# Scores of the first four head pairs as float32 products on TensorE, with the ranks of the plan set anew

## The chip, the cores and the metric

One Trainium2 chip, one NeuronCore. The time is the device time of one execution in microseconds (us); the kernel before is given as the median of three runs. Engines: PE (TensorE) does matrix products and PEld its weight loads, DVE (VectorE) and ACT (ScalarE) work element by element, POOL (GpSimd) helps, SP issues DMAs. PE writes only to PSUM; DVE and ACT read it from there.

## The reference

q, k and v are float32 of shape (4, 8, 1152, 64): 4 batches, 8 heads, 1152 positions, 64 numbers each. The weights come as float64, 512 x 2048 and 2048 x 512.

```python
q_pool = q.reshape(B, H, S // 2, 2, D).mean(axis=3)            # 576 queries
scores = 1 / np.sqrt(D) * np.matmul(q_pool, k.transpose(0, 1, 3, 2))
scores = scores - np.max(scores, axis=-1, keepdims=True)
attn = np.exp(scores)
attn = attn / (np.sum(attn, axis=-1, keepdims=True) + 1e-09)
attn_out = np.matmul(attn, v)                                  # (4, 8, 576, 64)
x = attn_out.transpose(0, 2, 1, 3).reshape(B * S, H * D)       # 2304 x 512
h = x @ w_in                                                   # 2304 x 2048
g = h * (1.0 / (1.0 + np.exp(-1.702 * h)))
out = g @ w_out                                                # 2304 x 512
```

## The kernel before

Two heads make a pair P, so there are 16 pairs, 4 to a batch. A pair has 9 score tiles n of 128 queries by 1152 keys: 4 of head A, 4 of head B, and one (L) with 64 queries of each. Each tile goes through S (scores on PE, L580), M (row maximum and copy out of PSUM on DVE, L589) and E (exp with row sum on ACT, L596). One PSUM area `s` of three banks holds the scores, so S of the next tile waits for M of this one.

Precision comes from splitting. For every pair the largest |q| and |k| are found (`q_max` L406, `k_max` L412), brought to all rows by a transpose on PE, a maximum, and a product (`rows_max` L421, `spread` L425 and L426, `to_all` L429), and turned into scales that are powers of two (`qk_scale`, L250 to L256 and L437). q and k times their scale are cut into two float16 parts (`q_hi`, `k_hi` on ACT by L240; `q_lo` L448, `k_lo` L462 on DVE), and both are transposed by a DMA each (`q_tr` L473, `k_tr` L469). A score tile is then six float16 products of 384 columns.

After E there are two ways. Seven pairs (WHOLE: 0, 1, 2, 3, 6, 10, 14) stay in float32: nine transposes of 128x128 on PE through the banks `o0` and `o1` (X, `w_tr` L655), three evictions of 384 columns (Y, `w_ev`, L240), float32 products with v (`w_pv` L678), and a product that spreads the reciprocal sums along rows (`w_rows` L693, evicted by `w_spread`). The other nine cut the probabilities into two float16 parts (H on ACT, L on DVE at L616), transpose them by DMA (T, `p_tr` L630) and multiply in float16 (`pv` L643). Row sums get 1e-9 added (D, `denom` L601) and are inverted (R, `recip` L608), tile by tile.

Beside this the float64 weights are decoded in 32 pieces (`w_load`, `w_exp`, `w_low` L275, `w_bits` L279, `w_sign` L285, `w_mul` L289 on POOL, `w_sum` L294 on PE) through four `raw` buffers, and cut into float16 parts (`w_hi`, `w_lo` L312). The MLP runs over nine blocks of 256 rows with eight steps each: 24 products of 256 columns (h, L840), tanh, gate and split on ACT and DVE, 12 products of 512 columns (o, L876). A block needs the x of all four pairs of its batch; the tanh of the first block waits for all 32 weight pieces.

The order on all engines is worked out before the launch by a list planner (class Plan): each task has an engine, a cost in us, the tasks and buffers that it waits for, and a rank; among tasks that could start within `wait` us of the earliest one on an engine, the lowest rank goes first. `rank` holds the numbers that the ranks are made of, `movable` names kinds of tasks that may go to a second engine. The plan only fixes the order of instructions per engine; on the chip they wait for semaphores.

Of the kernel before, what the change touches and what calls it, by code (L numbers as in the profile page):

```python
# [21 lines left out]
class Plan:  # L22
# [15 lines left out]
    def add(self, name, eng, cost, rank, fn, after=(), take=(), use=(), dma=0.0, or_on=None, two=False):  # L38
        t = dict(name=name, rank=rank, fn=fn, take=list(take), dma=dma, two=two)
# [19 lines left out]
    def order(self):  # L59
# [12 lines left out]
        dma_free, lock, out = 0.0, 0.0, []  # L72
# [17 lines left out]
        while len(out) < len(self.tasks):  # L90
# [13 lines left out]
            cost = t["on"][eng]  # L104
            end = free[eng] = self.run_pe(s, cost) if eng == "PE" else s + cost
# [12 lines left out]
            for h in heirs.get(t["name"], ()):  # L118
                for e in h["on"]:
                    at = free[e] if e == eng == "PE" and not t["dma"] else seen  # L120
# [10 lines left out]
def kernel(  # L131
# [38 lines left out]
    WHOLE = (0, 1, 2, 3, 6, 10, 14)  # L170


    rank = dict(
        w1=65.6152, w1_rate=1.375516, w2=121.4095, w2_rate=0.041077, w1_cut=225.7614,
        w1_cut_rate=0.0234, w2_cut=136.659, w2_cut_rate=1.877582, v_max=117.7693, load=-0.0554,
        prep=1.4415, max=-3.6165, exp=-72.3267, p_hi=0.5721, p_lo=1.4833, pv=17.7389, x=63.2346,
        recip=-10.7343, w_tr=2.6166, w_ev=-51.7958, g=-131.2414, pv_b=-6.1948, max_b=8.382,
        p_lo_b=-88.3476, prep_b=-1.6277, v=7.8426,
    )
    movable = dict(DVE=("x", "w_exp", "w_sign", "w_hi"), POOL=("denom",))  # L180
    wait = dict(PE=0.051, ACT=0.076, DVE=0.083, POOL=3838.461)
# [29 lines left out]
    w_r = const.tile([128, NJ * len(WHOLE), 2], F32, name="w_r")  # L211
# [111 lines left out]
    for i in range(32):  # L323
# [5 lines left out]
        plan.add(("w_load", i), "SP", 0.6, r - 2, lambda i=i: w_load(i), take=[("raw", raw)], dma=1.8)  # L329
        plan.add(  # L330
            ("w_exp", i), "ACT", act(512), r, lambda e, i=i: w_exp(e, i), [("w_load", i)], use=[raw], two=True,
# [20 lines left out]
    for c in range(8):  # L352
        for h in range(2):
# [9 lines left out]
            plan.add(("w_lo", c, h), "DVE", dve(1024), r, lambda c=c, h=h: w_lo(c, h), [("w_hi", c, h)], two=True)  # L363
# [9 lines left out]
    ORDER = [("A", 0), ("A", 1), ("B", 0), ("B", 1), ("A", 2), ("A", 3), ("B", 2), ("B", 3), ("L", 0)]  # L373
# [26 lines left out]
    def q_add(g, eng):  # L400
        raw, s = T["qraw", g.P], new("qs", ("qs", g.P), [128, NJ, D], F32)
        eng.tensor_tensor(out=s, in0=raw[:, :, 0, :], in1=raw[:, :, 1, :], op=ALU.add)
# [14 lines left out]
    def rows_max(m, key):  # L417
# [3 lines left out]
        nc.tensor.transpose(ps[0:n, 0:128], m, idf)  # L421

    def spread(key, n):
        r, d = new("cm", ("cm",) + key, [2, 1], F32), new("cd", ("cd",) + key, [2, 2], F32)
        nc.vector.tensor_reduce(out=r[0:n], in_=T[key][0:n, 0:128], axis=AX.X, op=ALU.max)  # L425
        nc.vector.tensor_scalar(out=d[0:n, 0:n], in0=idf[0:n, 0:n], scalar1=r[0:n], scalar2=None, op0=ALU.mult)  # L426

    def to_all(key, n):
        nc.tensor.matmul(  # L429
            out=T[key][:, 128:128 + n], lhsT=ones_f[0:n], rhs=T[("cd",) + key][0:n, 0:n], start=True, stop=True  # L430
        )

# [41 lines left out]

    def vm_load(b, i):
# [12 lines left out]
    def vm_scale(b):  # L488
        pow2(T["vma", b][:, 128:129], 2.0 ** -40, 14, s_v[:, b:b + 1], i_v[:, b:b + 1])
# [21 lines left out]
    for b in range(B):  # L511
        first = min(g.n0 for g in pairs if g.b == b)
        for i in range(H):
            r = first - 16 + 1.5 * i if b else -2 + i * 0.25
            plan.add(("vm_load", b, i), "SP", 0.6, r - 2, lambda b=b, i=i: vm_load(b, i),
# [9 lines left out]
        plan.add(("rows_max",) + va, "PE", 0.1, r - 20, lambda b=b, va=va: rows_max(T["vm", b], va), [("vm_row", b)],  # L525
                 take=[("tr", va)])
        plan.add(("spread",) + va, "DVE", 0.35, r - 20, lambda va=va: spread(va, 1), [("rows_max",) + va], use=[va])
        plan.add(("to_all",) + va, "PE", 0.15, r - 20, lambda va=va: to_all(va, 1), [("spread",) + va], use=[va])
        plan.add(("vm_scale", b), "DVE", 0.8, r, lambda b=b: vm_scale(b), [("to_all",) + va], use=[va])

    for g in pairs:
# [7 lines left out]
        plan.add(("q_load", G), "SP", 2.4, n0 + rank["load"], lambda g=g: q_load(g), gate, take=[("qraw", qr)], dma=1.4)  # L539
        plan.add(("k_load", G), "SP", 1.2, n0 + rank["load"] + 0.1, lambda g=g: k_load(g), gate, take=[("kraw", kr)], dma=2.2)  # L540
        plan.add(("q_add", G), pe[0], dve(576) if now else gps(576), r, lambda g=g, e=pe[1]: q_add(g, e),
                 [("q_load", G)], take=[("qs", qs)], use=[qr], two=True)
        plan.add(("q_max", G), "DVE", dve(576), r, lambda g=g: q_max(g), [("q_add", G)], use=[qs])
        plan.add(("k_max", G), "DVE", dve(1152), r, lambda g=g: k_max(g), [("k_load", G), ("q_max", G)], use=[kr])
        qa = ("qka", G)
        plan.add(("rows_max",) + qa, "PE", 0.1, r - 20, lambda g=g, qa=qa: rows_max(T["qk", g.P], qa),
                 [("q_max", G), ("k_max", G)], take=[("tr", qa)])
        plan.add(("spread",) + qa, "DVE", 0.35, r - 20, lambda qa=qa: spread(qa, 2), [("rows_max",) + qa], use=[qa])
        plan.add(("to_all",) + qa, "PE", 0.15, r - 20, lambda qa=qa: to_all(qa, 2), [("spread",) + qa], use=[qa])
        plan.add(("qk_scale", G), "DVE", 0.8, r, lambda g=g: qk_scale(g), [("to_all",) + qa], use=[qa])  # L550
        plan.add(("q_hi", G), "ACT", act(1152, ptr=1), r, lambda e, g=g: q_hi(e, g), [("qk_scale", G)],
                 take=[("qn", qk)], use=[qs], two=True, or_on=on("q_hi", DVE=dve(1152, fast=True)))
        plan.add(("q_lo", G), "DVE", dve(576), r, lambda g=g: q_lo(g), [("q_hi", G)], use=[qs, qk], two=True)
        plan.add(("k_hi", G), "ACT", act(1152, ptr=1), r, lambda e, g=g: k_hi(e, g), [("qk_scale", G)],
                 take=[("kn", kn)], use=[kr], two=True, or_on=on("k_hi", DVE=dve(1152, fast=True)))
        plan.add(("k_lo", G), "DVE", dve(1152), r, lambda g=g: k_lo(g), [("k_hi", G)], use=[kr, kn], two=True)
        plan.add(("q_tr", G), "SP", 3.0, r, lambda g=g: q_tr(g), [("q_lo", G)], take=[("qT", qt)], use=[qk], dma=2.7)
        plan.add(("k_tr", G), "SP", 3.0, r, lambda g=g: k_tr(g), [("k_lo", G)], take=[("kT", kt)], use=[kn], dma=2.7)
# [7 lines left out]
        plan.add(("v_lo", G), "DVE", dve(1152), r, lambda g=g: v_lo(g), [("v_hi", G)],  # L566
                 use=[("vraw", G), ("vhl", G)], two=True)


    def scores(n):  # L570
        g, kind, t = tile_of[n]
        ps = new("s", ("s", n), [128, 3, 512], F32, psum)
# [24 lines left out]

    def denom(e, n):
        whole = tile_of[n][0].whole
        r = T["rc", n] = w_r[:, WHOLE.index(n // NJ) * NJ + n % NJ, :] if whole else new("rc", ("rc", n), [128, 2], F32)  # L600
        (nc.vector if e == "DVE" else nc.gpsimd).tensor_scalar(  # L601
            out=r[:, 0:1], in0=T["sum", n], scalar1=1e-9, scalar2=1.0 if whole else 2.0 ** -15,
            op0=ALU.add, op1=ALU.mult,
# [30 lines left out]
    def pv(g, u, part):  # L634
# [5 lines left out]
        for c in range(KR):  # L640
            for a in range(2):
                pt, o = (T["pt", g.P, "AB"[a], u], 0) if u < 2 else (T["pt", g.P, "L", 0], 64 * a)
                nc.tensor.matmul(  # L643
                    out=ps[64 * a:64 * (a + 1), 0:w], lhsT=T["vhl", g.P][:, a, c, m],
# [374 lines left out]
```

## Time and profile before

| what | value |
|---|---|
| median of three runs | 840.02 us (838.73 to 841.5) |
| span of the profiled execution, first to last instruction | 841.4 us |
| PE busy | 779.7 us (93%) |
| PEld busy | 516.3 us (61%) |
| DVE busy | 628.5 us (75%) |
| ACT busy | 574.6 us (68%) |
| POOL busy | 99.7 us (12%) |

The profile is of one execution, whose time is not given apart from its span; the span lies 1.4 us above the median of the runs. Busy times are records of instructions. The matrix products overlap in their pipeline, so PE counts as busy from the start of a product until its end is out, and a PE that is shown busy is not always at its full rate: how far apart two products start says more.

### The profile page before, as it was taken

The numbers are of one execution on the slowest core, as the hardware profiler recorded it, in microseconds if no ns is written. First come the engines' busy times: TensorE is split into PE (matmuls) and PEld (weight loads), VectorE is DVE, ScalarE is ACT, GpSimd is POOL, SyncE is SP. The second block draws the span as 40 slices with busy tenths as digits, with TensorE's granted clock in tenths as the row PEclk, the third lists the DMA queues.
The fourth block names the chain that finished last, engine by engine and source line by source line (L and its number), as shares of the span: only waits on it lengthen the run. The fifth ranks groups of instructions, "written<-read, shape, count | busy, mean of one in ns | idle before, by whom it ended". The sixth has DMA issues, their size and how long they took to land.

```text
span 841.4 us, 16413 instructions
## 1 busy us (share of the span) xinstructions
PE 779.7 (93%) x6565; PEld 516.3 (61%) x6565; DVE 628.5 (75%) x1160; ACT 574.6 (68%) x892; POOL 99.7 (12%) x141
## 2 busy tenths in 40 slices
PE   1689999998979999999998999999989999999997
PEld 0356555556656765666665766666667657666664
DVE  5788998999999769798998589988975683222221
ACT  3588989998867778677766787786868774232322
POOL 1233232230001100010100010101110000000000
PEclk9999999999999999999999999999999999999999
DMA  8876965819999918999999559999893383000001
GB/s 284 247 187 209 250 151 166 210 61 205 216 172 210 215 49 168 181 185 209 215 212 212 111 109 198 174 202 199 158 216 67 43 174 80 14 13 13 17 10 25
DMA packets 296364, 126.96 MB, mean 151 GB/s; under 512 B 267360, under 2 KB 277600, under 8 KB 296288
## 3 DMA queue, kind: packets, MB, share of 16 engines
q1 hardware_dynamic: 296288, 125.92, 69.3%
q8 instruction: 51, 0.84, 0.4%
q14 instruction: 25, 0.20, 0.1%
HBM read 54.53 MB, written 4.72 MB: 70 GB/s over the span
## 4 chain that ended last, share of the span: by engine, by line
PE 64%; DVE 16%; DMA 9%; ACT 6%; issue 4%; SPq 1%; POOL 0%; ACTq 0%; DVEq 0%; POOLq 0%
PE h L840 17%; PE o L876 16%; PE s L580 11%; PE pv L678 6%; PE o L655 6%; PE pv L643 5%; DVE p L589 4%; DMA pt<-hl 4%; DVE hl L616 3%; DMA vst<-in_v_dram 2%; ACT p L596 2%; DMA ptl<-hl 2%; ACT pt L240 1%; DVE gf L854 1%; DVE raw L279 1%
## 5 line engine op out<-in xcount | busy, mean ns | idle before, releaser
L596 ACT ACTIVATE p<-p,nm 128x1152 f32<-128x1152 f32 x144 | 180.5, 1254 | 56.5 <-DVE p L589 42.8
L589 DVE TENSOR_SCALAR_CACHE_REDUCE p<-s,e_s 128x1152 f32<-128x1152 f32 x144 | 202.9, 1409 | 21.4 <-PE s L580 20.0
L876 PE MATMUL o<-wbuf,g 128*128 128x512 f16 x864 | 202.7, 379 | 0.0
L840 PEld LDWEIGHTS <-wbuf 128*128 128x128 f16 x1728 | 167.0, 98 | 46.8 <-issue 14.9
L580 PE MATMUL s<-kT,qT 128*128 128x384 f16 (+1 forms) x960 | 167.4, 330 | 11.2 <-DVE p L589 8.3
L876 PEld LDWEIGHTS <-g 128*128 128x128 f16 x864 | 83.4, 98 | 86.2 <-issue 1.7
L580 PEld LDWEIGHTS <-qT 128*128 128x128 f16 (+1 forms) x960 | 83.8, 101 | 73.3 <-issue 27.9
L840 PE MATMUL h<-x16a,wbuf 128*128 128x256 f16 x960 | 116.5, 273 | 7.9 <-DVE gf L854 7.9
L616 DVE SCALAR_TENSOR_TENSOR hl<-p,rc,hl 128x1152 f16<-128x1152 f32 x81 | 116.4, 1438 | 9.6 <-ACT hl L240 9.2
L240 ACT ACTIVATE hl<-p,rc 128x1152 f16<-128x1152 f32 x81 | 100.8, 1246 | 19.7 <-DMA pt<-hl 13.3
L854 DVE SCALAR_TENSOR_TENSOR gf<-th,h 128x512 f32<-128x512 f32 x72 | 49.3, 685 | 84.1 <-ACT th L848 83.8
L848 ACT ACTIVATE th<-h,t_s 128x512 f32<-128x512 f32 x72 | 49.0, 681 | 90.7 <-PE h L840 90.6
L655 PE MATMUL o<-idf,p 128*128 128x128 f32 x567 | 90.1, 285 | 6.8 <-ACT pt L240 5.9
L840 PE MATMUL h<-wbuf 128*128 128x256 f16 x768 | 91.7, 273 | 2.7 <-DVE gf L854 2.7
L240 ACT ACTIVATE pt<-o 128x384 f32<-128x384 f32 x168 | 77.3, 489 | 17.9 <-PE o L655 17.2
L655 PEld LDWEIGHTS o<-idf,p 128*128 128x128 f32 x567 | 65.4, 144 | 35.6 <-ACT pt L240 16.5
L643 PEld LDWEIGHTS <-vhl 128*64 128x64 f16 x1458 | 60.3, 111 | 14.3 <-issue 8.6
L865 DVE SCALAR_TENSOR_TENSOR g<-gf,g 128x512 f16<-128x512 f32 x72 | 50.4, 700 | 21.7 <-ACT g L240 21.7
L240 ACT ACTIVATE g<-gf 128x512 f16<-128x512 f32 x72 | 44.9, 624 | 31.6 <-DVE gf L854 29.7
L678 PE MATMUL pv<-pt,vraw 128*64 128x256 f32 x504 | 62.9, 387 | 0.0
L643 PE MATMUL pv<-pt,vhl 128*64 128x256 f16 x972 | 59.1, 274 | 1.0 <-DMA pt<-hl 1.0
L678 PEld LDWEIGHTS pv<-pt,vraw 128*64 128x64 f32 x504 | 32.8, 136 | 20.2 <-issue 7.4
(89 smaller groups left out, 642.5 us busy)
## 6 DMA issues: line engine op xcount, KB each, us to landing
kraw<-in_k_dram SPq DMA_DIRECT2D x32, 288.0 KB, 4.1
vst<-in_v_dram SPq DMA_DIRECT2D x32, 288.0 KB, 4.2
vraw<-in_v_dram SPq DMA_DIRECT2D x32, 288.0 KB, 3.5
qraw<-in_q_dram SPq DMA_DIRECT2D x32, 256.0 KB, 4.0
raw<-in_moe_w_in_dram SPq DMA_DIRECT2D x16, 512.0 KB, 6.0
raw<-in_moe_w_out_dram SPq DMA_DIRECT2D x16, 512.0 KB, 4.4
out_dram<-osb SPq DMA_DIRECT2D x16, 256.0 KB, 2.5
pt<-hl SPq DMA_TRANSPOSE x72, 5.4
```

The source lines that it names most:

```text
L240: nc.scalar.activation(out=out, in_=in_, func=ACTF.Copy, scale=1.0 if scale is None else scale)
L580: nc.tensor.matmul(out=ps[m, c, 0:384], lhsT=st, rhs=T["kT", g.P][:, o:o + 3].rearrange("p r c -> p (r c)"), start=(l == 0), stop=(l == 1),)
L589: nc.vector.tensor_scalar(out=p, in0=T["s", n][:, :, 0:384], scalar1=e_s[:, g.P:g.P + 1], scalar2=None, op0=ALU.mult, op1=ALU.min, accum_o ...
L596: nc.scalar.activation(out=p, in_=p, func=ACTF.Exp, bias=T["nm", n], scale=-1.0, accum_out=sm)
L616: nc.vector.scalar_tensor_tensor(out=t[:, 1, :], in0=T["p", n].rearrange("p c f -> p (c f)"), scalar=T["rc", n][:, 1:2], in1=t[:, 0, :], o ...
L643: nc.tensor.matmul(out=ps[64 * a:64 * (a + 1), 0:w], lhsT=T["vhl", g.P][:, a, c, m], rhs=pt[:, l * KR + c, o:o + w], start=(part == 0 and ...
L655: nc.tensor.transpose(ps[:, 128 * i:128 * (i + 1)], T["p", n][:, c, 128 * i:128 * (i + 1)], idf)
L678: nc.tensor.matmul(out=ps[64 * a:64 * (a + 1), 0:w], lhsT=T["vraw", g.P][:, a, c], rhs=pt[:, c, o:o + w], start=(c == 0), stop=(c == KR - 1),)
L840: nc.tensor.matmul(out=h[:, e, :], lhsT=w1(2 * j + e, l, kk), rhs=x_rhs(blk, m, kk), start=(kk == 0 and l == 0 and m == 0), stop=(kk == KD ...
L854: nc.vector.scalar_tensor_tensor(out=gf, in0=T["th", blk, j], scalar=1.0, in1=T["h", blk, j].rearrange("p e n -> p (e n)"), op0=ALU.add, o ...
L865: nc.vector.scalar_tensor_tensor(out=g[:, 1].rearrange("p e n -> p (e n)"), in0=T["gf", blk, j], scalar=2.0 ** -16, in1=g[:, 0].rearrange( ...
L876: nc.tensor.matmul(out=o, lhsT=g[:, l, e, 128 * t:128 * (t + 1)], rhs=w2(fc, m), start=(fc == 0 and l == 0 and m == 0), stop=(fc == KFF - ...
```

## The change

For pairs 0 to 3 (WIDE) the scores are float32 products of the unscaled sums of q and the unscaled k. Both are transposed on PE: 9 blocks of k and 9 of q, each 128x128, in six groups (`qk_tr`, through the banks `o0` and `o1`), evicted by ACT or DVE (`qk_ev`). A block holds two neighbouring 64-row pieces, one in the lower and one in the upper half of the partitions; q is laid out so that each piece of q is found in either half. A tile is three products, each with 64 of TensorE's 128 rows: 512 keys from one half, 512 from the other, and the 128 left over (`scores_wide`); tile L has six. The maxima, scales, splits and DMA transposes of these four pairs go; their score factor is the constant -1/16.

Further: the maxima of the other pairs reach all rows by products with a broadcast operand and one reduction (`rows_max`, `max_all` in place of `spread` and `to_all`). In the seven WHOLE pairs the sums are inverted in groups of 4, 4 and 1 tiles (`w_denom`, `w_recip`) instead of tile by tile. The first load of k is issued from ACT's queue, not SP's. All of `rank`, `wait` and `movable` and several costs of the planner are other numbers, and the planner gets a cost for a change of TensorE's tile shape between tasks (SWITCH, `mode`).

```diff
-    HOP = dict(PE=0.28, ACT=0.16, DVE=0.14, POOL=0.15, SP=0.2)
-    DMA_IN, DMA_OUT = 0.3, 1.3
+    HOP = dict(PE=0.25, ACT=0.16, DVE=0.14, POOL=0.15, SP=0.2)
+    DMA_IN, DMA_OUT, SWITCH = 0.3, 2.0, 0.095
...
+    WIDE = (0, 1, 2, 3)
+    BLOCKS = ((0, 2, 4, 6, 1, 3, 5, 7, 8), (1, 3, 5, 7, 2, 4, 6, 8, 0))
...
-    movable = dict(DVE=("x", "w_exp", "w_sign", "w_hi"), POOL=("denom",))
-    wait = dict(PE=0.051, ACT=0.076, DVE=0.083, POOL=3838.461)
+    movable = dict(DVE=('w_spread', 'w_ev', 'k_hi', 'qk_ev', 'x_hi'), POOL=('denom',))
+    wait = dict(PE=0.051, ACT=0.333, DVE=0.116, POOL=0.952)
...
-            nc.sync.dma_start(out=t[:, a], in_=k[g.b, 2 * g.pr + a].rearrange("(p r) d -> p r d", r=KR))
+            e = nc.sync if g.P else nc.scalar
+            e.dma_start(out=t[:, a], in_=k[g.b, 2 * g.pr + a].rearrange("(p r) d -> p r d", r=KR))
...
-        nc.tensor.transpose(ps[0:n, 0:128], m, idf)
+        for i in range(n):
+            nc.tensor.matmul(
+                out=ps[:, 128 * i:128 * (i + 1)], lhsT=m[:, i:i + 1].to_broadcast([128, 128]), rhs=idf,
+                start=True, stop=True,
+            )
...
+    PARTS = (("k", 0, 4), ("q", 0, 4), ("k", 4, 5), ("q", 8, 9), ("k", 5, 9), ("q", 4, 8))
+
+    def qk_tr(g, i):
+        what, lo, hi = PARTS[i]
+        ps = new(f"o{i % 2}", ("qkp", g.P, i), [128, 512], F32, psum)
+        for j in range(lo, hi):
...
+            nc.tensor.transpose(ps[:, 128 * (j - lo):128 * (j - lo + 1)], src, idf)
+
+    def qk_ev(e, g, i):
...
+        copy(e, d, T["qkp", g.P, i][:, 0:128 * (hi - lo)])
...
+    def scores_wide(n):
+        g, kind, t = tile_of[n]
+        ps = new("s", ("s", n), [128, 3, 512], F32, psum)
+        kT, qT = T["kT", g.P], T["qT", g.P]
+
+        def part(half, bank, a, first, last):
+            m = slice(64 * a, 64 * a + 64) if kind == "L" else slice(0, 128)
+            h, j = slice(64 * half, 64 * half + 64), NJ - 1 if kind == "L" else 4 * a + t
+            nc.tensor.matmul(
+                out=ps[m, bank, 0:128 * (last - first)], lhsT=qT[h, (j - half) % NJ, m],
+                rhs=kT[h, first:last].rearrange("p j c -> p (j c)"), start=True, stop=True,
+            )
+
+        if kind == "L":
...
+        else:
+            a = int(kind == "B")
+            for half in range(2):
+                part(half, half, a, 5 * a, 5 * a + 4)
+            part(a, 2, a, 4, 5)
...
+            ("S", n), "PE", (1.5 if kind == "L" else 1.07) if g.wide else 0.975, n, lambda n=n: scores(n),
+            ([("qk_ev", g.P, last)] if g.wide else [("k_tr", g.P), ("q_tr", g.P)])
```

## Rows read from the trace of the kernel before

**Rows 1.** The page: busy time of each engine, and PE's busy tenths in 40 slices.

```profile
PE 779.7 (93%) x6565; PEld 516.3 (61%) x6565; DVE 628.5 (75%) x1160; ACT 574.6 (68%) x892; POOL 99.7 (12%) x141
...
PE   1689999998979999999998999999989999999997
```

**Rows 2.** Stretches: length, then PE, PEld, DVE, ACT, POOL busy (us, records).

```profile
0.00:29.60 29.60, 6.08 (x14) 2.06 (x15) 17.01 (x30) 9.65 (x12) 8.57 (x13) 1.00 0.92 272
29.60:175.70 146.10, 136.71 (x1030) 84.97 (x1028) 134.52 (x296) 131.65 (x247) 40.13 (x50) 1.00 0.70 198
...
220.00:700.00 480.00, 459.69 (x4171) 310.97 (x4170) 398.21 (x707) 355.69 (x522) 45.48 (x72) 1.00 0.87 168
700.00:841.40 141.40, 136.67 (x1016) 92.08 (x1013) 35.80 (x51) 40.34 (x62) 0.67 (x1) 0.99 0.06 18
```

**Rows 3.** The second of these stretches, row maxima (L589) alone; each tile leaves two records.

```profile
29.60:175.70 146.10, 50.99 (x72) 1.00 0.70 198
```

**Rows 4.** Timeline from 0 to 30 us: start, length, engine, line, what, idle before.

```profile
5.27 0.76 DVE L402 TENSOR_TENSOR qs<-qraw 128x576 f32<-128x576 f32 x1 [4.13 <-DMA qraw<-in_q_dram]
...
8.24 1.35 DVE L412 TENSOR_REDUCE qk<-kraw 128x1 f32<-128x1152 f32 x1 [1.43 <-DMA kraw<-in_k_dram]
...
12.11 0.19 DVE L437 TENSOR_SCALAR e_s<-i_qk 128x1 f32<-128x1 f32 x1
...
22.66 3.33 SPq L469 DMA_TRANSPOSE kT<-kn  x1
...
27.53 2.08 PE L580 MATMUL s<-kT,qT 128*128 128x384 f16 x6 [1.85 <-DMA kT<-kn]
...
29.65 1.42 DVE L589 TENSOR_SCALAR_CACHE_REDUCE p<-s,e_s 128x1152 f32<-128x1152 f32 x1 [3.45 <-PE s L580]
```

**Rows 5.** Groups of instructions, all of the span: count, busy us, mean ns.

```profile
L240 ACT ACTIVATE pt<-o 128x384 f32<-128x384 f32 x168 | 77.3, 489 | 17.9 <-PE o L655 17.2
...
L462 DVE SCALAR_TENSOR_TENSOR kn<-kraw,s_qk,kn 128x1152 f16<-128x1152 f32 x16 | 23.3, 1454 | 0.6 <-ACT kn L240 0.5
...
L412 DVE TENSOR_REDUCE qk<-kraw 128x1 f32<-128x1152 f32 x16 | 21.5, 1342 | 1.4 <-DMA kraw<-in_k_dram 1.4
...
L240 ACT ACTIVATE kn<-kraw,s_qk 128x1152 f16<-128x1152 f32 x16 | 19.9, 1243 | 0.0
...
L448 DVE SCALAR_TENSOR_TENSOR qn<-qs,s_qk,qn 128x576 f16<-128x576 f32 x16 | 13.0, 810 | 1.5 <-ACT qn L240 1.4
...
L406 DVE TENSOR_REDUCE qk<-qs 128x1 f32<-128x576 f32 x16 | 11.9, 743 | 4.3 <-POOL qs L402 4.3
...
L608 DVE RECIPROCAL w_r<-w_r 128x1 f32<-128x1 f32 x63 | 9.9, 157 | 0.6
...
L425 DVE TENSOR_REDUCE cm<-tr 2x1 f32<-2x128 f32 x16 | 4.4, 273 | 0.9 <-PE tr L421 0.9
...
L240 ACT ACTIVATE xt<-tr 128x256 f32<-128x256 f32 x7 | 2.7, 386 | 0.3
```

**Rows 6.** The chain that ended last, 71 to 86 us: start, length, what.

```profile
72.08 1.45 PE pv L678 x12
73.52 1.08 PE s L580 x6
74.60 0.66 PE o L655 x6
...
80.79 0.97 PE s L580 x6
...
84.12 0.45 PE h L294
```

**Rows 7.** Of the weight pieces (L289) and the first MLP products (L840): first and last start.

```profile
L289 POOL TENSOR_TENSOR wbuf<-raw x32: 1036/1042/1487, 12.1 to 183.5; 128x512 f32<-128x512 f32 x32
...
L840 PE MATMUL h<-x16a,wbuf x960: 269/273/283, 185.8 to 831.1; 128*128 128x256 f16 x192
```

**Rows 8.** The chain that ended last, 220 to 300 us: its longest piece.

```profile
229.40 8.01 DMA ptl<-hl
```

More of the change, by code (lines that the diff above doesn't have):

```diff
@@ L119, in order @@
                 for e in h["on"]:
-                    at = free[e] if e == eng == "PE" and not t["dma"] else seen
+                    at = free[e] if e == eng and (e == "PE" or h["name"][0] == t["name"][0] == "T") else seen
                     ready[id(h), e] = max(ready[id(h), e], at)
@@ L371, in __init__ @@
             self.whole = P in WHOLE
-    ORDER = [("A", 0), ("A", 1), ("B", 0), ("B", 1), ("A", 2), ("A", 3), ("B", 2), ("B", 3), ("L", 0)]
+            self.wide = P in WIDE
+            self.block = BLOCKS if self.wide else (range(9), range(9))
+    ORDER = SLOTS
     pairs, tile_of, num = [], [], {}
@@ L538 @@
         kt, qt = ("kT", G), ("qT", G)
[L539 to L540 removed]
+        plan.add(("q_load", G), "SP", 2.3, n0 + rank["load"], lambda g=g: q_load(g), gate, take=[("qraw", qr)], dma=1.4)
+        plan.add(("k_load", G), "SP" if G else "ACT", 1.2, n0 + rank["load"] + 0.1, lambda g=g: k_load(g), gate, take=[("kraw", kr)], dma=2.2)
@@ L548 @@
[L548 to L557, printed above, removed]
@@ L565 @@
                  take=[("vhl", ("vhl", G))], use=[("vraw", G)], or_on=on("v_hi", DVE=dve(1152, fast=True)), two=True)
-        plan.add(("v_lo", G), "DVE", dve(1152), r, lambda g=g: v_lo(g), [("v_hi", G)],
+        plan.add(("v_lo", G), "DVE", dve(1152) + 0.06, r, lambda g=g: v_lo(g), [("v_hi", G)],
                  use=[("vraw", G), ("vhl", G)], two=True)
+    def scores_wide(n):
[8 more added lines that the diff above has]
+                rhs=kT[h, first:last].rearrange("p j c -> p (j c)"), start=True, stop=True,
+            )
+        if kind == "L":
+            part(1, 2, 1, 4, 5)
+            for a in range(2):
+                for half in range(2):
+                    part(half, half, a, 5 * a, 5 * a + 4)
+            part(0, 2, 0, 4, 5)
+        else:
+            a = int(kind == "B")
+            for half in range(2):
+                part(half, half, a, 5 * a, 5 * a + 4)
+            part(a, 2, a, 4, 5)
     def scores(n):
         g, kind, t = tile_of[n]
+        if g.wide:
+            return scores_wide(n)
         ps = new("s", ("s", n), [128, 3, 512], F32, psum)
@@ L683, in w_rows @@
     def w_rows(g, u):
-        ps = new("tr", ("wr", g.P, u), [128, 3, 128], F32R, psum).bitcast(F32).rearrange("p a b -> p (a b)")
-        for i in range(2 if u < 2 else 1):
-            for a in range(2):
-                n = g.n0 + g.tiles.index(("L", 0) if u == 2 else ("AB"[a], 2 * u + i))
-                r = T["rc", n][:, 1:2].to_broadcast([128, 64])
-                o, m = ps[:, 128 * i:128 * (i + 1)], idf
-                if u == 2:
-                    o, m = ps[:, 0:64], idf[:, 64 * a:64 * (a + 1)]
-                nc.tensor.matmul(out=o[64 * a:64 * (a + 1)], lhsT=r, rhs=m, start=True, stop=True)
+        ps = new("tr", ("wr", g.P, u), [128, 384], F32, psum)
+        r = w_r[:, w_cols(g, u)]
+        if u < 2:
+            for i in range(2):
+                for a in range(2):
+                    nc.tensor.matmul(
+                        out=ps[64 * a:64 * (a + 1), 128 * i:128 * (i + 1)],
+                        lhsT=r[:, 2 * a + i:2 * a + i + 1].to_broadcast([128, 64]), rhs=idf, start=True, stop=True,
+                    )
+            return
+        for a in range(2):
+            nc.tensor.matmul(
+                out=ps[64 * a:64 * (a + 1), 0:64], lhsT=r.to_broadcast([128, 64]), rhs=idf[:, 64 * a:64 * (a + 1)],
+                start=True, stop=True,
+            )
     def w_spread(e, g, u):
@@ L783 @@
         for part in range(3):
-            cost = (3 * w / 600 if g.whole else 9 * max(w, 68) / 2400) + 0.1
+            cost = 3 * (w / 600 + 0.01) if g.whole else 9 * max(w / 2400 + 0.002, 0.032)
             plan.add(
@@ L792 @@
             wr = ("wr", g.P, u)
-            plan.add(("wr", g.P, u), "PE", 0.13 if u == 2 else 0.5, r, lambda g=g, u=u: w_rows(g, u),
-                     [("R", e) for e in mine] + wr_last, take=[("tr", wr)])
+            plan.add(("w_denom", g.P, u), "DVE", 0.09, n + rank["recip"], lambda e, g=g, u=u: w_denom(e, g, u),
+                     [("E", e) for e in mine], or_on=on("denom", POOL=0.27))
+            plan.add(("w_recip", g.P, u), "DVE", 0.09, n + rank["recip"], lambda g=g, u=u: w_recip(g, u),
+                     [("w_denom", g.P, u)])
+            plan.add(("wr", g.P, u), "PE", 0.12 if u == 2 else 0.434, r, lambda g=g, u=u: w_rows(g, u),
+                     [("w_recip", g.P, u)] + wr_last, take=[("tr", wr)], mode=3)
             wr_last = [wr]
@@ L984 @@
         nc.vector.memset(ones_f, 1.0)
+        nc.vector.memset(e_s, -1.0 / 16)
         for t in qn:
```

166 lines of the change are left out of this document (109 added, 57 removed).

## The prediction, made before the changed kernel was run

> **What bounds the kernel now.** I read the busy shares and slices first. PE is recorded busy for 93% of the span, and its slices are full except for the first two, 1 and 6 tenths [rows 1]. A share like that hides where time can be won, so the table of stretches comes next [rows 2]. The reader is to see four different regimes in it.
>
> Up to 29.6 us PE has 6.1 us of records, and the timeline says why: the first tile of pair 0 waits for a chain through every engine. q is there at 5.3 us, k at 8.2, the scales at 12.1, then come the splits, and the DMA transpose of k is issued at 22.7; PE gets its first score at 27.5 and DVE the first maximum at 29.65 [rows 4].
>
> From 29.6 to 175.7 us the tiles of pairs 0 to 3 pass: 72 records of row maxima, two to a tile, so 36 tiles in 146.1 us [rows 3]. There DVE has 134.5 us of records (92%), ACT 131.7 (90%) and PE 136.7 (94%) [rows 2]. All three are close together, so no engine may be relieved without asking for the next.
>
> From 220 to 700 us PE is recorded busy 95.8% and idle for 20.3 us, with DVE at 83%. There the chain shows waits of PE's consumers for DMA transposes of probabilities, 8.0 us in its longest piece [rows 8], but little PE time is lost by them. After 700 us the MLP alone is left, at 96.7% [rows 2]. Nothing of the change touches that tail; time that is won before it moves it forward whole.
>
> **PE's own work in the second stretch.** Records of PE overlap, so I price work by the spacing in the chain where PE runs without a gap [rows 6]: six transposes 0.66 us (0.11 each), a float16 score tile 0.97, the same tile right after `w_pv` 1.08, one `w_pv` part (12 records) 1.45, a weight sum 0.45. The difference 1.08 - 0.97 = 0.11 is what PE loses when the shape of the tile on the array changes. The code has, for 36 tiles, 324 transposes (35.6 us), 36 score tiles at 1.0 (36), 24 full `w_pv` parts (34.8) and the short parts of four L tiles (estimate 3.5), about 25 weight sums (11.3; 32 are made between about 12 and 184 us [rows 7]) and about 6 for `w_rows` and small things. Sum 127 us of 146.1, or 87%. So PE still has 19 us of slack there that the records do not show.
>
> **What the change does to the start.** Gone are maxima, scales, splits and both DMA transposes of pair 0. Left: k now leaves from ACT's queue beside q, and I take both as landed by 6 us (q was at 5.3, k, issued behind it, at 8.2 [rows 4]). The first S needs four groups of transposes and their evictions through two banks. PE is at its slow rate: the first six products took 2.08 us against 0.97 later [rows 4, 6], so a group of four costs 0.9 us; an eviction of 512 columns is 0.59 us on ACT (386 ns for 256 columns and 489 for 384 [rows 5], so 0.8 ns a column). Groups 0 and 1 (k and q, four blocks each) with their evictions end at 7.8 and 8.7; groups 2 and 3 wait for those banks and end at about 9.6. S then takes 2.1 us at the slow rate and M starts at 12. The two issues of k that move to ACT's queue cost nothing there: ACT is busy 9.65 of the first 29.6 us [rows 2], and behind them stands only what waits for the same loads; if ACT's queue were late, k would land as before, which the upper bound covers. Bounds: 10 if evictions and transposes overlap fully, 16 if k lands at 8.2 as before and each step waits for the one before. I take 12, near the rows of loads that landed first: **-17.6 us** against 29.65.
>
> **The four pairs, DVE and ACT.** Per pair DVE loses 0.743 + 1.342 + 0.810 + 1.454 us and seven small operations of 0.273 at most, 1.4 together (estimate), which is 5.75 us; ACT loses two splits of 1.24 each, 2.5 [rows 5]. For pairs 1 to 3, which fall in this stretch, -17.3 and -7.5. Inverting in groups takes three reciprocals a pair for nine: 6 x 0.157 x 4 = 3.8 us, and about 1 us of additions. New are evictions of 2304 columns a pair: four of 0.59 and two of 0.28 (the line through the same rows), 2.9 us, 8.8 for three pairs. Work on weights that filled the empty first 29.6 us comes later: DVE and ACT had 17.0 and 9.7 us there [rows 2], of which 8 and 4 were pair 0's preparation and the table load; some 11 of the remaining 15 us must be caught up. Sum over both engines: 266.2 - 24.8 - 4.8 + 8.8 + 11 = 256.4, and since `w_ev` and `qk_ev` may now go to either, 128 each; at the 91% seen here 141 us. That is 5 us under the 146.1.
>
> **The four pairs, PE.** A wide tile has 1152 columns in float32. `w_pv` gives the rate: a part is 6 products of 256 columns on half of the array's columns, two running side by side, 1.45 us [rows 6], so four passes' worth, 1.67 ns a column on the full array (6 x 256 / 2 x 1.67 = 1.28, and the change of shape on top). If the two halves of rows run beside each other as those halves of columns do, 640 columns count and a tile costs 640 x 1.67 = 1.07 us. If not, 1152 columns, 1.92 us. The nearest row is `w_pv`, also float32 and also two tiles of the array side by side, so I take 1.07. Transposes before and after have another shape than S now, where they had the same: two changes of shape a tile, 2 x 0.11 = 0.22. So 36 x (1.07 + 0.22 - 1.0) = +10.4 us, +1.6 for the L tiles, and 54 transposes of q and k in this stretch, +5.9; the small products of the old maxima give back 1.5. PE needs 127 + 16 = 143 us. **PE becomes the bound of the stretch.** At the 95.8% of the third stretch it takes 149 us: **+3 us** against 146.1. Bounds: 141 (what DVE and ACT allow) and 181 (halves one after the other, below).
>
> A sentence of the Trainium skill speaks against 1.07: the page "TensorE: Matmul & The Clock Gate", section "Part 3: Packing small matmuls", says that products start and end strictly in program order. A float32 product leaves two records here, and if the second pass of one half stood in the queue ahead of the first of the other, the halves would overlap in part only. By that rule a tile would cost 1.28 to 1.49 us. The two records of `w_pv`'s neighbours would be under the same rule, and at 1.45 us for 12 records [rows 6] they do run side by side, so I give it a small chance (below).
>
> **The rest.** Pairs 4 to 15 keep float16 scores. Their `rows_max` is two full float32 products (0.43) where a transpose and a small product stood: +0.1 us or so a pair, **+1 us** in all, and one less DVE step. What the new order of pairs 4 to 15 and the MLP does can't be read from the trace of before; its bounds are the 20.3 us of recorded PE idle [rows 2] to win and as much to lose by orders that let PE wait for transposes. The planner now reckons a DMA as landing 0.7 us later than it did, which leaves more room ahead of waits like [rows 8]; I take **-4 us**, a fifth of that idle.
>
> **Sum.** 841.4 - 17.6 + 3 + 1 - 4 = 823.8 us of span. The span of the profile lies 1.4 us above the median of the runs, so 822.4; forecast 822.5, that is 2.1% less.
>
> **Rivals.**
> - More is won (15%). `w_ev` on either engine lets PE run at 98% in the four pairs (146 us, nothing added), and half of the idle of the third stretch goes (-10). For it: DVE is at 92% there, and its evictions wait in line. Against: one PSUM area `s` still alternates between S and M. 841.4 - 17.6 + 0 + 1 - 10 - 1.4 = 813.
> - The MLP does not start earlier (10%). The tanh of its first block waits for the 32nd weight piece, which started at 183.5, and its first product ran at 185.8 [rows 7]. If the weights keep their pace, PE lacks that work for up to 14.6 us (-17.6 + 3) and has only tiles that come early, about three; I price the loss at 9: 831.5.
> - The halves overlap in part (8%): 1.28 to 1.49 a tile, some 0.3 more on 36 tiles, +11 on a PE that is the bound, /0.958: 834.
> - The halves of the rows run one after the other (5%), the case on the other side. Place: S of the first 36 tiles; price 1.92 - 1.07 = 0.85 each, 31 us. PE then needs 174 us, at 95.8% 181: +32 against the forecast, 854, slower. It decides from about 1.5 us a tile: then what the start gives back is gone (14.6 + 3 = 17.6 us over 36 tiles is 0.49 on 1.07).
> - The new order lets PE wait where it didn't (7%): the idle of the third stretch doubles, +20 instead of -4: 846.
>
> **How the numbers follow.** The forecast has 55%, its own range 815 to 831 by the bounds on the first maximum (10 to 16) and on the order (-10 to +4). Over all cases the range is 805 to 838: it holds the forecast, the larger gain, and the two small losses, and leaves out the serial halves and most of the bad order. About 0.3% (2.5 us) is what a measurement here can tell from nothing, so faster means below 837.5. Faster: 55 + 15 + 10 + 8 less the tails that reach up, 82%; same 6%; slower 12%.
>
> **What would show it.** Right: the first record of row maxima at 10 to 14 us; 36 tiles of wide pairs in 145 to 153 us, with PE's records nearly gapless and DVE under 90%; float32 products of two halves starting within a few ns of each other, a tile in about 1.07 us; the first MLP product near 171 us; from there to the end as long as the 655.6 us of before, or a few us less. Wrong: score tiles spaced by 1.3 us or more when nothing else holds PE; the first maximum later than 16 us; the MLP still starting at 185; or gaps of PE between 220 and 700 us that sum to clearly more than 20 us.

## The result and the profile after

The changed kernel takes 816.1 us (815.5 to 818.6, four runs) against 840.2: the ratio is 0.972, 95% interval 0.969 to 0.975. The forecast of 822.5 was 6.4 us too high; the time lies in the range of 805 to 838.

The page first: busy time of each engine, and PE's slices [rows 1].

```profile
PE 790.1 (97%) x6633; PEld 530.5 (65%) x6633; DVE 634.0 (78%) x1093; ACT 546.1 (67%) x834; POOL 107.7 (13%) x143
...
PE   6999999999899999999999999999999999999997
```

PE has 10 us more of records in a span that is 24.6 us shorter, and the first slices are no longer nearly empty. The start, as timeline rows that answer to [rows 4]:

```profile
4.36 1.09 PE L495 MATMUL o<-idf,kraw 128*128 128x128 f32 x4 [4.36 <-DMA kraw<-in_k_dram]
...
6.86 0.76 DVE L412 TENSOR_TENSOR qs<-qraw 128x576 f32<-128x576 f32 x1 [5.70 <-DMA qraw<-in_q_dram]
...
11.59 2.21 PE L621 MATMUL s<-kT,qT 64*128 64x512 f32 x6
...
13.84 1.42 DVE L664 TENSOR_SCALAR_CACHE_REDUCE p<-s,e_s 128x1152 f32<-128x1152 f32 x1 [1.94 <-PE s L621]
```

k is there at 4.4 us now, q at 6.9, and the first row maximum comes at 13.84 instead of 29.65. The row maxima alone, by stretches (72 records are 36 tiles) [rows 3]:

```profile
13.80:170.80 157.00, 51.12 (x72) 1.00 0.57 179
170.80:816.80 646.00, 153.13 (x216) 1.00 0.70 139
```

So the wide pairs take 157.0 us where they took 146.1, and pair 4 begins only 4.9 us earlier than before; from there to the end it is 646.0 us instead of 665.7 (841.4 - 175.7). The greater part of the gain, 19.7 of 24.6 us, appears after the pairs that the change is about. The stretches of pairs 0 to 3, 4 to 7, 8 to 11 and 12 to 15 in the changed kernel (length; then PE, PEld, DVE, ACT and POOL busy):

```profile
13.80:170.80 157.00, 152.67 (x1085) 91.26 (x1087) 148.30 (x281) 134.44 (x238) 48.51 (x51) 1.00 0.57 179
170.80:333.90 163.10, 156.91 (x1423) 108.75 (x1420) 150.72 (x258) 119.52 (x172) 16.75 (x28) 0.99 0.87 173
333.90:500.90 167.00, 164.38 (x1514) 113.22 (x1513) 150.71 (x258) 122.70 (x176) 20.56 (x33) 1.00 0.93 189
500.90:658.50 157.60, 155.84 (x1447) 108.93 (x1446) 135.45 (x227) 113.62 (x166) 17.66 (x23) 1.00 0.86 162
```

And the later three in the kernel before:

```profile
175.70:351.30 175.60, 163.55 (x1457) 109.87 (x1456) 155.87 (x282) 137.00 (x200) 18.20 (x25) 1.00 0.83 164
351.30:524.50 173.20, 165.86 (x1505) 111.22 (x1503) 146.56 (x267) 126.16 (x183) 16.31 (x27) 1.00 0.92 179
524.50:687.90 163.40, 159.46 (x1475) 108.99 (x1475) 130.33 (x227) 121.97 (x179) 14.92 (x24) 1.00 0.81 155
```

In the wide pairs PE is recorded busy 97.2%, DVE 94.5% and ACT 85.6%; that PE is their bound has to come from the runs below. In pairs 4 to 15 its idle time (length less PE) fell from 12.1 + 7.3 + 3.9 = 23.3 us to 6.2 + 2.6 + 1.8 = 10.6.

The weights and the first MLP product [rows 7]:

```profile
L296 POOL TENSOR_TENSOR wbuf<-raw x32: 1032/1042/1716, 12.9 to 136.1; 128x512 f32<-128x512 f32 x32
...
L946 PE MATMUL h<-x16a,wbuf x960: 269/273/283, 178.2 to 806.5; 128*128 128x256 f16 x192
```

The last weight piece starts 47 us earlier, the MLP only 7.6 us earlier.

### The profile page after: what moved, and what is told of

It reads as the page before. It is cut to its first block, busy times and chain, and to the rows that moved or that the text cites. A ratio compares the mean times of both kernels' runs of the same rounds, so it can differ in the third digit from the quotient of the medians.

```text
span 816.8 us, 16478 instructions
## 1 busy us (share of the span) xinstructions
PE 790.1 (97%) x6633; PEld 530.5 (65%) x6633; DVE 634.0 (78%) x1093; ACT 546.1 (67%) x834; POOL 107.7 (13%) x143
## 4 chain that ended last, share of the span: by engine, by line
PE 58%; DVE 16%; DMA 12%; issue 7%; ACT 2%; SPq 2%; POOL 2%; POOLq 0%; DVEq 0%; ACTq 0%
PE o L982 15%; PE h L946 15%; PE s L650 7%; PE pv L771 6%; PE o L748 6%; DMA pt<-hl 5%; PE pv L736 4%; DVE hl L709 4%; DVE p L664 3%; PE s L621 3%; DMA qraw<-in_q_dram 2%; DMA raw<-in_moe_w_in_dram 2%; DMA kraw<-in_k_dram 2%; DVE g L971 1%; DVE gf L960 1%
## 5 line engine op out<-in xcount | busy, mean ns | idle before, releaser
L982 PE MATMUL o<-wbuf,g 128*128 128x512 f16 x864 | 204.2, 379 | 1.1 <-DVE g L971 1.1
L982 PEld LDWEIGHTS <-g 128*128 128x128 f16 x864 | 83.3, 98 | 85.6 <-DVE g L971 2.0
L650 PE MATMUL s<-kT,qT 128*128 128x384 f16 (+1 forms) x720 | 123.3, 326 | 2.3 <-DVE p L664 2.0
L650 PEld LDWEIGHTS <-qT 128*128 128x128 f16 (+1 forms) x720 | 63.2, 100 | 45.7 <-issue 8.9
L748 PE MATMUL o<-idf,p 128*128 128x128 f32 x567 | 85.7, 281 | 1.8 <-ACT pt L247 1.2
L748 PEld LDWEIGHTS o<-idf,p 128*128 128x128 f32 x567 | 62.5, 141 | 25.0 <-issue 8.0
L736 PEld LDWEIGHTS <-vhl 128*64 128x64 f16 x1458 | 62.5, 112 | 12.8 <-issue 6.5
L736 PE MATMUL pv<-pt,vhl 128*64 128x256 f16 x972 | 61.6, 278 | 3.2 <-DMA pt<-hl 3.1
L247 ACT ACTIVATE pt<-o 128x384 f32<-128x384 f32 x101 | 46.5, 486 | 14.8 <-PE o L748 11.3
L621 PE MATMUL s<-kT,qT 64*128 64x512 f32 (+3 forms) x240 | 49.1, 521 | 1.4 <-DVE p L664 1.3
```

Source lines behind the costliest of these rows:

```text
L247: nc.scalar.activation(out=out, in_=in_, func=ACTF.Copy, scale=1.0 if scale is None else scale)
L621: nc.tensor.matmul(out=ps[m, bank, 0:128 * (last - first)], lhsT=qT[h, (j - half) % NJ, m], rhs=kT[h, first:last].rearrange("p j c -> p (j ...
L650: nc.tensor.matmul(out=ps[m, c, 0:384], lhsT=st, rhs=T["kT", g.P][:, o:o + 3].rearrange("p r c -> p (r c)"), start=(l == 0), stop=(l == 1),)
L736: nc.tensor.matmul(out=ps[64 * a:64 * (a + 1), 0:w], lhsT=T["vhl", g.P][:, a, g.block[a][c], m], rhs=pt[:, l * KR + c, o:o + w], start=(pa ...
L748: nc.tensor.transpose(ps[:, 128 * i:128 * (i + 1)], T["p", n][:, c, 128 * i:128 * (i + 1)], idf)
L982: nc.tensor.matmul(out=o, lhsT=g[:, l, e, 128 * t:128 * (t + 1)], rhs=w2(fc, m), start=(fc == 0 and l == 0 and m == 0), stop=(fc == KFF - ...
```

## The experiments

The table gives the ratio to the kernel before (runs of the same chip) with its interval, and from the profile the first row maximum, the time of pairs 0 to 3 and 4 to 7 (from the first maximum of one pair to that of another), and from pair 4 to the end of the span, all in us. The last four columns are of one profiled execution each. Those of the changed kernel, e11 and e12 took 2.5, 3.5 and 3.8 us more than the medians of their kernels, those of e2 and e14 1.6 and 2.2 us less; the span before lies 1.2 us above its median, and every other span is some 1.8 us shorter than the time of its execution. So differences between the columns are certain to a few us only.

| kernel | ratio | first max. | pairs 0-3 | pairs 4-7 | pair 4 to end |
|---|---|---|---|---|---|
| before | 1 | 29.6 | 146.1 | 175.6 | 665.7 |
| changed | 0.972 (0.969 to 0.975) | 13.8 | 157.0 | 163.1 | 646.0 |
| e1_narrow | 1.032 (1.028 to 1.036) | 29.2 | 159.4 | 167.5 | 673.3 |
| e2_old_ranks | 0.991 (0.988 to 0.994) | 14.6 | 153.7 | 175.6 | 660.2 |
| e3_old_costs | 1.025 (1.022 to 1.027) | 14.2 | 167.0 | 196.0 | 678.8 |
| e7_weights_late | 1.020 (1.017 to 1.023) | 14.1 | 155.1 | 201.3 | 684.0 |
| e8_narrow_guard | 1.009 (1.006 to 1.013) | 27.8 | 162.1 | 166.9 | 654.0 |
| e9_late_guard | 0.988 (0.985 to 0.990) | 13.7 | 155.5 | 178.1 | 658.8 |
| e10_costs_guard | 0.990 (0.987 to 0.993) | 14.1 | 163.2 | 169.3 | 653.5 |
| e6_warm_after | 0.978 (0.975 to 0.980) | 14.1 | 156.5 | 163.5 | 649.9 |
| e11_old_no_lo | 0.991 (0.987 to 0.994) | 15.4 | 155.2 | 179.5 | 664.0 |
| e12_new_no_lo | 0.972 (0.968 to 0.975) | 14.3 | 158.7 | 163.8 | 645.4 |
| e13_cuts_early | 0.977 (0.974 to 0.980) | 14.3 | 160.7 | 163.4 | 646.6 |
| e14_held | 0.985 (0.982 to 0.988) | 24.9 | 156.7 | 160.1 | 642.2 |

**Scores or order?** The first four runs each take one part of the change back.

```diff
-    WIDE = (0, 1, 2, 3)
+    WIDE = ()
```

> The changed kernel with WIDE empty: pairs 0 to 3 score in split float16 as before, while the new ranks, planner costs, grouped inversions and the broadcast maxima stay. Theory A (what was predicted: the gain is the 15.8 us by which the first row maximum came earlier, handed on to the end): the first maximum goes back to 28 to 30 us and the time to 830 to 838. Theory B (most of the gain is the new order: in the changed kernel pair 4 began only 4.9 us earlier and the end came 24.6 us earlier): the first maximum also goes back to 28 to 30, but the time is 818 to 826, and PE's records between 220 and 700 us stay near 471 us against 460 before.

865.4 us, far above both numbers; PE's records between 220 and 700 us are 463.8 us, nearer the 460 of before than theory B's 471.

In e2, `rank`, `movable` and `wait` are those of the kernel before:

```diff
-    wait = dict(PE=0.051, ACT=0.333, DVE=0.116, POOL=0.952)
+    wait = dict(PE=0.051, ACT=0.076, DVE=0.083, POOL=3838.461)
...
```

> The changed kernel with rank, wait and movable of the kernel before; the wide scores and the planner's new costs stay. Theory A: the first maximum stays near 14 us and the time at 818 to 826. Theory B: 828 to 838, with PE's records between 220 and 700 us near 460.

832.1 us, in theory B's range, though PE's records between 220 and 700 us are 469.0, not near its 460. The first maximum comes 0.8 us later than in the changed kernel. The wide pairs take 153.7 us with 128.2 us of records on DVE (first row below). From pair 4 to the end it takes 660.2 us, 5.5 less than before and 14.2 more than the changed kernel. PE is idle 15.5 us in pairs 4 to 7 (second row), against 6.2.

```profile
14.60:168.30 153.70, 149.53 (x1072) 90.23 (x1072) 128.19 (x245) 131.68 (x253) 45.94 (x45) 1.00 0.57 180
168.30:343.90 175.60, 160.06 (x1427) 108.47 (x1426) 153.50 (x265) 134.47 (x196) 16.75 (x21) 0.99 0.82 162
```

e3 has the old costs in the planner:

```diff
-    HOP = dict(PE=0.25, ACT=0.16, DVE=0.14, POOL=0.15, SP=0.2)
+    HOP = dict(PE=0.28, ACT=0.16, DVE=0.14, POOL=0.15, SP=0.2)
-    DMA_IN, DMA_OUT, SWITCH = 0.3, 2.0, 0.095
+    DMA_IN, DMA_OUT, SWITCH = 0.3, 1.3, 0.0
```

> The changed kernel with three planner costs as before (hop after PE 0.28, DMA landing 1.3 instead of 2.0, no cost for a change of TensorE's tile shape); the ranks are the new ones. If what the new order wins rests on these costs (the theory behind the -4 us of the prediction), PE waits more for DMA transposes between 220 and 700 us and the time is 822 to 832. If the ranks alone carry it: 815 to 820.

And e7 has one other rank:

```diff
-        w1=211.958642, w1_rate=358.198269, w2=247.385733, w2_rate=0.279118, w1_cut=1077.998449,
+        w1=211.958642, w1_rate=358.198269, w2=385.0, w2_rate=0.279118, w1_cut=1077.998449,
```

> The changed kernel with one rank number changed (w2 385 for 247), so that the last weight pieces and half of the weight cuts on DVE stand as late among the tiles as they did before. Theory of displacement (the four wide pairs took 157 us, not 149, because weight work was pulled forward into them, and pairs 4 to 7 got shorter by it): the 36 wide tiles take 148 to 153 us, pairs 4 to 7 take 168 to 175 against 163.1, and the end is within 3 us of the changed kernel's 816. Rival (TensorE is the bound of the wide pairs, whatever DVE does): the 36 tiles still take 155 to 159 us. If the early weights are themselves what wins the time at the end: 822 or more.

e3 took 859.8 us, outside both of its ranges. e7 took 855.5: that is "822 or more", and its wide pairs take 155.1 us, as the rival on TensorE said, but pairs 4 to 7 take 201.3, which nothing had foreseen. In both one pair takes almost 70 us: pair 6. PE's timeline in e7 shows why.

```profile
269.54 1.14 PE L650 MATMUL s<-kT,qT 128*128 128x384 f16 x6
...
285.61 2.75 PE L982 MATMUL o<-wbuf,g 128*128 128x512 f16 x12
...
301.46 5.45 PE L982 MATMUL o<-wbuf,g 128*128 128x512 f16 x24
306.75 0.49 PE L748 MATMUL o<-idf,p 128*128 128x128 f32 x3
307.69 0.87 PE L748 MATMUL o<-idf,p 128*128 128x128 f32 x6 [0.45 <-ACT osb L990]
...
310.73 1.14 PE L650 MATMUL s<-kT,qT 128*128 128x384 f16 x6
```

No score tile runs from 269.5 to 310.7. The float32 transposes of pair 6 (L748) need the PSUM banks `o0` and `o1`, and a block of the MLP adds up its result (L982) in these two from its first step to its eighth. Block 1 took them at 260 us, a moment before pair 6, and pair 6 could only go on when the block was evicted (L990). Before and in the changed kernel the block comes after the pair (its first o at 321.9 and at 305.0). In e1 it happens to pair 14 with block 5, for 37 us.

**The banks taken out of the comparison.** One wait in the plan puts the blocks behind the pairs. The kernel before and the changed one stand in this order already: in both, blocks 1, 3 and 5 begin their o after the last transpose of pairs 6, 10 and 14.

```diff
+                if i == j == 0 and blk in (1, 3, 5):
+                    before += [("Y", 9 * (2 * blk + 4) + t, c) for t in range(9) for c in range(3)]
```

> Narrow scores with the new ranks again (WIDE empty), and a wait added to the plan: blocks 1, 3 and 5 of the MLP start their second product (o) only after the float32 transposes of pairs 6, 10 and 14, which use the same PSUM banks o0 and o1. The changed kernel's order has this already and is not changed by the wait. Theory of the banks (in e1_narrow block 5 held o0 and o1 from 640 to 679 us in the middle of pair 14, which waited 37 us): pair 14 takes 39 to 47 us instead of 81, and the time falls to 832 to 845. If e1_narrow's 865 came from elsewhere (scores in float16 with ranks made for wide ones): above 855. What is then left between this and 816 is what the wide scores are worth under the new ranks: theory A of e1 says 830 or more, theory B 826 or less.

> Late weights (w2 385) with the same added wait. Theory of the banks: in e7 block 1 held the banks from 260 to 307 us and pair 6 waited 42 us; with the wait pair 6 takes 40 to 48 us and the time is 815 to 826. Displacement: the sum over pairs 0 to 7 (first maximum of pair 0 to that of pair 8) is within 5 us of the changed kernel's 320.1, whatever the split. If early weights are themselves worth time: 826 or more.

> Old planner costs (hop 0.28, landing 1.3, no cost of shape changes) with the same added wait. Theory of the banks: pair 6 takes 40 to 48 us, not 69, and the time is 815 to 828; what is left above 816 is what the planner's costs are worth. If the costs matter by themselves (more waits for DMA transposes): 828 or more.

846.3, 829.7 and 832.1 us: the wait gives back 19, 26 and 28 us of what e1, e7 and e3 had lost, and pair 6 takes 45.6 and 42.0 us in e9 and e10, pair 14 40 in e8. The banks were the cause of the long pairs. All three times stay above what their optimistic theory said; e9 and e10 lie where their rivals put them (826 or more, 828 or more), e8 just above the 845 of the banks and on theory A's side (830 or more). e8 against the changed kernel shows the wide scores under the new ranks: 27.1 us of span (30.2 by the medians), 14.0 at the first maximum, 5.1 in pairs 0 to 3 and 8.0 later. With the old ranks (before against e2, which also has the new costs, maxima and inversions) it is 12.9 us of span, but 6.7 by the medians. e9 shows that late weights save 1.5 us in the wide pairs and cost 12.8 from pair 4 on.

**Is it DVE's time?** e9 suggests that weight cuts in pairs 4 to 7 cost their DVE time. So eight of them are left out (the low half of w2 is then missing from the output), once in e2, where they stand late, and once in the changed kernel, where they stand early:

```diff
+        if c >= 4:
+            return
         nc.vector.scalar_tensor_tensor(
...
-                out=o, lhsT=g[:, l, e, 128 * t:128 * (t + 1)], rhs=w2(fc, m),
+                out=o, lhsT=g[:, l, e, 128 * t:128 * (t + 1)], rhs=w2(fc, 0),
```

> e2_old_ranks (old ranks, wide scores; 832), with the low half of w2 not made: its eight cuts on DVE (1.3 us each, between 207 and 262 us) are left out, and the second product takes the high half in its place, in the same shapes; the order of all else is unchanged. Theory (in pairs 4 to 7 DVE is the bound, and weight cuts that stand there lengthen them): pairs 4 to 7 go from 175.6 to 163 to 168 us and the time to 820 to 826. Rival (the difference there comes from the order of other things): they stay within 3 us of 175.6, the time 829 or more.

> The changed kernel (816) with the same eight cuts left out; there they stand between 160 and 234 us, five of them before pair 4. Theory (TensorE is the bound of the wide pairs, so DVE work costs little there): the four wide pairs stay within 3 us of 157.0, pairs 4 to 7 lose at most 5 of their 163.1, the time is 811 to 816. Rival (a cut costs its DVE time wherever it stands): the time falls by as much as from e2 to e11.

833.2 and 816.4 us: nothing is gained in either. The theory falls. In e11 DVE has 9.2 us less of records in pairs 4 to 7 than in e2, and the stretch does not shrink; it is 4.0 us longer, which the rival did not say either:

```profile
170.50:350.10 179.60, 162.76 (x1428) 109.36 (x1426) 144.28 (x258) 135.08 (x196) 16.28 (x21) 0.97 0.82 159
```

The granted clock is 0.97 in this row: TensorE stood at 1.2 GHz for 10.2 us of it, against 3.4 in e2. Even with all of these 10.2 us at twice the rate the stretch would be some 174.5 us, above the 163 to 168 of the theory.

e13 pulls the last cuts forward as well:

```diff
-        w1_cut_rate=0.001511, w2_cut=102.436204, w2_cut_rate=0.00457, v_max=1699.580189, load=-316.66678,
+        w1_cut_rate=0.001511, w2_cut=100.0, w2_cut_rate=1.0, v_max=1699.580189, load=-316.66678,
```

> The changed kernel with the last weight cuts pulled forward too (w2_cut 100 with rate 1; all sixteen stand before tile 38, where two stood at tiles 45 and 49), with the wait of e8 on the banks. If early cuts go on paying: pairs 4 to 7 take 158 to 162 us instead of 163.1 and the time is 811 to 816. If the changed kernel's order is a lucky one that any move spoils, as the runs so far suggest: 819 to 830.

821.2 us, no better than the changed kernel and in the range of the second guess, that any move spoils the order. Pairs 4 to 7 stay at 163.4; the wide pairs take 160.7 for 157.0. Of these 3.7 us pair 0 has 2.5 (37.4 for 34.9), and in the profiled execution the clock rose only at 22.2 us, so this is no sure effect of the cuts. e12 has the same late rise and the same 37.4.

**Is time at the start handed on?** Two kernels put products on a constant ahead of everything on PE, 34 in e6, 320 in e14; all else is in the same order.

```diff
+        dummy = psum.tile([128, 512], F32, tag="o0", name="o0", bufs=1)
+        for i in range(320):
+            nc.tensor.matmul(out=dummy[:, 0:128], lhsT=ones, rhs=ones, start=True, stop=True)
```

> The changed kernel with 34 products of 128 columns on a constant ahead of everything else on TensorE, while it waits for k (its results are not used). The granted clock then rises before 13.4 us; if by 9 us, the first maximum comes at 11.5 to 12.8 instead of 13.84. If time won at the start is handed on whole: 814 to 815.3. If it is lost on the way (DVE and ACT are the bound of the first pairs): 815.5 to 817.

> The changed kernel with 320 products on a constant ahead of everything on TensorE, so that its first transposes come at about 20 us, not 4.4, with the clock up; DVE and ACT are free to go ahead with weights. The prediction took time won at the start to be handed on whole: then the time is 828 to 833 (16 later, less some 2 to 4 for the clock). If it is absorbed, because the start of pair 4 or the tail is bound by something else: 816 to 823.

e6 took 821.5 us, above both of its numbers, and its first maximum came at 14.1, no earlier. The rows show the products, four transposes, and PE idle for 2.36 us:

```profile
1.05 3.53 PE L1096 MATMUL o<-ones 128*128 128x128 bf16 x34 [1.05 <-DVE ones L1089]
4.69 0.63 PE L495 MATMUL o<-idf,kraw 128*128 128x128 f32 x4
7.68 1.12 PE L495 MATMUL o<-idf,qs 128*128 128x128 f32 x4 [2.36 <-DVE qs L412]
```

The clock had risen (0.63 us for four transposes, 1.09 in the changed kernel) and was gone again when q came (1.12). The 5 us that the kernel is slower by are not explained by 0.3 us at the start; instructions that stand in the same order on every engine can still meet other waits, and in pairs 8 to 11 this run took 171.2 us for 167.0. So differences of some 4 us between orders are not to be read as causes here.

e14 took 827.8 us, a ratio of 0.985, at the lower end of "handed on". PE began 16 us later and had the clock; the first maximum came 11.1 us later than in the changed kernel, pair 4 10.8 later (181.6), pair 8 7.8, pair 12 10.1, and the span ended 7.0 later; in the medians the kernel is 11.7 us slower. The wide pairs, compared with the changed kernel's 157.0, show no slack that would absorb a late start:

```profile
24.90:181.60 156.70, 152.69 (x1087) 91.33 (x1088) 148.25 (x282) 135.43 (x240) 49.27 (x51) 1.00 0.55 173
```

## Why the prediction was right, and where it was not

**The start: right.** -15.8 us where -17.6 was forecast, inside its bounds of 10 to 16 for the first maximum. k came first and q 0.9 us later than taken, and q has the longer way. e8, which keeps all else that changed at the start, has its first maximum at 27.8: 14.0 of the 15.8 us are the wide scores.

**Handed on: right for the greater part.** e14 passes on 10.8 of 11.1 us to pair 4 and 7 to 12 to the end.

**TensorE becomes the bound of the wide pairs: right; the size was off.** 157.0 us, forecast 149: +10.9 for +3. PE is recorded busy 97.2%, and DVE's load does not set the length: 128.2 us of DVE records in e2's 153.7 us and 148.3 in 157.0 here; cuts left out (e12, with 4 us less on DVE) shorten nothing. Three things can be told. A full wide tile occupies PE for 1.28 us until the next product starts (median of the 32, from the records' starts), and with the 0.11 for the change of shape ahead of it 1.39, not 1.29: +3.2 us over 32 tiles. The four L tiles went the other way: 1.23 us each, 1.34 with the change, where the forecast had 0.4 more than for a full tile, 1.69: -1.4. About six more weight sums stand in the stretch, at 0.45 [rows 6] +2.7. The rest, 3.4 us, is not accounted for. The sum for DVE and ACT was too small as well: 148.3 + 134.4 = 282.7 us of records for 256.4, so DVE is at 94.5%, not under 90. In e2, with the old ranks, it is 259.9: the new ranks put more work into these pairs.

**The halves run side by side: right.** The starts of the six records of one tile, in us: 28.911, 28.918, 29.445, 29.451, 29.874, 29.983. The first two start 7 ns apart and, by the spacing, are the first passes of the two halves; the next two, 0.53 us later and 6 ns apart, are the second passes; the last two are the 128 columns left over. The Trainium skill's page "TensorE: Matmul & The Clock Gate" (section "Part 3: Packing small matmuls") says that starts stay in program order. The records do not give a pass's place in the program, so they cannot test that sentence; the partial overlap that I drew from it did not come, since by their starts the passes of the halves alternate. Without the change of shape a tile takes 1.28 - 0.11 = 1.17 us, for 1.07 forecast and 1.28 to 1.49 by that rival; it and the one with serial halves are out.

**The MLP's start: wrong in its reason.** It came 7.6 us earlier, not 14.6, yet the weights did not hold it: their last piece began at 136.1. A block needs the x of pairs 0 to 3, and these ended later than forecast: pair 4's start moved 4.9.

**The rest of the order: the step that failed.** Predicted were -4 us for the new order of pairs 4 to 15 and the MLP and +1 for the new maxima (which no run has alone); measured from pair 4 to the end, -19.7. This term was taken as a fifth of PE's recorded idle in 220 to 700 us. That idle fell by 11.6, from 20.3 to 8.7 us, and from pair 4 to the end it fell by 13.5, from 28.8 to 15.3. PE's own work there is nearly the same: from the records' columns (columns / 2.4 GHz, doubled in float32, where the starts above are 0.42 us apart after 512 columns and 0.11 after 128; halved for half an array) it comes to some 592 us before and 595 after. So the time beyond work fell from 74 to 51 us, by 23, of which less than two thirds was visible as idle: a product's record runs on while the next one cannot start yet. The 20.3 us that I set as the bound on this gain were therefore no bound, though by luck the gain stayed just under them.

A small part of the rest can be named. From pair 4 to the end PE changes the shape of its tile 123 times, and 146 before (the small products of the old maxima not counted). Where no gap stands between two float32 records, such a change adds 94 ns between their starts (median), so 23 fewer are 2.2 us. The ranks do this, not the price in the plan: with the old ranks there are 150 changes (e2), without the price 122 (e10). About 7 us stay open.

What brought the gain is the order that the new ranks, `wait` and `movable` give. With the old ones 14.2 of the 19.7 us are lost by the spans. By the medians it is nearly all: e2 is 6.7 us faster than the kernel before, and its pair 4 begins 7.5 us earlier, so nothing is won after that. The order rests on more than them: 7.5 us are lost with the old costs (e10) and 12.8 with the weights late (e9), each time in an order worked out anew. It is not DVE's time for the cuts (e11, e12). The new order helps narrow scores too from pair 4 on: in e8 that part takes 654.0 us, 11.7 less than before. What makes e8 0.9% slower than the kernel before stands in pairs 0 to 3, 162.1 us for 146.1, where PE is idle for 22.8. Which instructions stand better in the changed order was not settled; orders in which 0.3 us at the start moves the end by some 4 us (e6) would need many runs for that.

Of the signs set beforehand, the first maximum and the starts of the halves came as written. The 36 tiles (157.0 us for 145 to 153), DVE's share, the first MLP product (178.2 for 171) and the time from there to the end (638.6 us for 655.6, 17.0 less and not a few) did not. None of the four signs of being wrong came, though a tile's 1.28 us is close to the 1.3 of the first.

The errors of +10.9 for +3 and of -19.7 for -3 have opposite signs, so it is luck that the sum came out within 6.4 us. The mechanism at the start was right; most of the net gain was where I had put little.

## What to carry to other kernels

Where an order has been worked out for one kernel, taking back a part of it and working the order out anew measures the order, not the part: look at the trace for one large gap (here 37 to 42 us, two PSUM banks held by a whole block) before reading a cause from the time. Time won ahead of a stretch whose bound engine is full is handed on; time taken from an engine that is not the bound there is not. And the recorded idle time of TensorE does not limit what a better order can win: here it fell by 13.5 us while the time beyond work fell by 23.

## What was not expected of the hardware

The granted clock of TensorE rose from 1.2 to 2.4 GHz at 13.4 us in the changed kernel and at 40.4 before, by the clock records of the two traces, so the earlier start also ended the slow rate 27 us earlier: pairs 0 to 3 ran wholly at 2.4 GHz, and for 10.8 us at 1.2 before. In e6 it rose at 4.2 us, fell at 7.6 after PE had stood idle from 5.3, and rose again at 14.4. In e8 it fell, among others, at 36.3 and at 84.1 us, each time for 6.8 us; PE had stood idle for 3.4 us from 34.4 and for 2.0 from 81.3.
